# A grouped 1x1 convolution on one core: wider block transposes with longer write runs, and loads cut into four transfers

## The chip, the cores and the metric

One core of a Trainium2 chip runs the whole program. Times are device microseconds (us) of one execution. A run is in state fast or slow where several executions of the same kernel show which it was, and unknown for a single look; a single look therefore carries no claim of a per cent or less here.

## The reference

The input is an image of 512x512 pixels with 192 channels in bf16. The channels form 4 groups of 48, and each group of each pixel is multiplied by its own 48x48 matrix.

```python
H = W = 512; G = 4; Cg = 48; C = 192; k = 1          # x: (1, 512, 512, 192), w: (1, 1, 4, 48, 48)
xg = xp.reshape(B, H + 2 * pad, W + 2 * pad, G, Cg)  # pad = 0
out = out + jnp.einsum('bhwgc,gcd->bhwgd', xg[:, i:i+H, j:j+W, :, :], w[i, j])
```

100.7 MB are read and 100.7 MB written, whatever the kernel does.

## The kernel before

The kernel gives TensorE the channels on the partitions, but a pixel's channels lie side by side in memory. So pixels are loaded onto the partitions, VectorE transposes them in blocks of 32x32 (`Q` in the kernel), TensorE multiplies, ScalarE copies the result from PSUM into the same ring, and the ring is stored. A "column" is 128 pixels. A "piece" of up to 128 columns is one load and one store, and the ring holds 512 columns.

```python
# SP: a piece goes in two transfers (u); r and b together are the 128 partitions, b neighbouring ones
src = pixels(xf, p).rearrange("(r u b n) c -> u r b (n c)", r=64, u=2, b=2)
half = p.size * C // 2
for u in range(2):
    sp.dma_start(region(p)[:, u * half:(u + 1) * half], src[u]).then_inc(ld_sem[p.i], 16)
...
# VectorE: 8 columns per transpose
src = columns(s).rearrange("p (w v) g n -> p w v (g n)", w=2, v=2)
dst = xT[s % NXT][:].rearrange("p (b w i v) -> p w v b i", w=2, i=2, v=2)
dve.transpose(dst, src).then_inc(t_done, 1)
...
# TensorE: 12 matmuls per step of 8 columns, into one of two halves of PSUM
ins = pe.matmul(o, lhsT=xs[:, at:at + 128], rhs=r, start=(b == 1), stop=(b == 2), skip_group_check=True)
...
# ScalarE: one copy per step; a piece is stored in rows of 12 KB once its last step is done
act.copy(dst, src).then_inc(o_done, 1)
```

The load and the transpose are coupled. The 128 pixel columns of a matmul must come out in the order of the store, so the order in which pixels are loaded onto the lanes fixes the addresses to which a transpose writes. Here the innermost write loop is `i`: two bf16 elements, two elements (4 bytes) apart, and the next pair starts 16 bytes after the first.

Of the kernel before, what the change touches and what calls it, by code (L numbers as in the profile page):

```python
# [10 lines left out]
C = GROUPS * CG  # L11
Q = 32
NQ = 128 // Q
HC = C // 2
BLK = HC // Q
STEP = 8
XT = STEP * C
SEG = NQ * CG
WT = 8 * SEG

BIG = 128
RCOLS = 512
HEAD = (8, 8, 16, 32, 64)
TAIL = (64, 32, 16, 8, 8)
NXT = 4
ST_DELAY = 1


class Waiter:
# [21 lines left out]

def plan_pieces(cols):
    sizes = []
    if cols >= sum(HEAD) + sum(TAIL):
        mid = cols - sum(HEAD) - sum(TAIL)
        sizes = list(HEAD) + [BIG] * (mid // BIG) + ([mid % BIG] if mid % BIG else []) + list(TAIL)
    else:
        sizes = [BIG] * (cols // BIG) + ([cols % BIG] if cols % BIG else [])
    pieces, c = [], 0
    while sizes:  # L60
        s = min(sizes[0], RCOLS - c % RCOLS)
        sizes[0] -= s
        if not sizes[0]:
            sizes.pop(0)
        pieces.append(Piece(len(pieces), c, s))
        c += s
    return pieces


def bass_standalone__grouped__vision_kernel(nc, x, w, out):  # L70
    B, H, W_, Cx = x.shape
    assert Cx == C and tuple(w.shape) == (1, 1, GROUPS, CG, CG)
    npix = B * H * W_
    assert npix % (128 * STEP) == 0, "the pixel count must be a multiple of 1024"

    cols = npix // 128
    NS = cols // STEP
    pieces = plan_pieces(cols)
    piece_of = {s: p for p in pieces for s in range(p.s0, p.s1)}
    first = {p.s0: p for p in pieces}  # L80
    last = {p.s1 - 1: p for p in pieces}

    xf = x.rearrange("b h w c -> (b h w) c")
    of = out.rearrange("b h w c -> (b h w) c")
    wr = w.rearrange("a b g c d -> (a b g c) d")

    def pixels(ap, p):
        return ap[128 * p.col:128 * (p.col + p.size), :]

    with ExitStack() as es:  # L90
        block = es.enter_context(nc.Block())
        ring = es.enter_context(nc.sbuf_tensor("ring", [128, RCOLS * C], BF16))
        xT = [es.enter_context(nc.sbuf_tensor(f"xT{i}", [128, XT], BF16)) for i in range(NXT)]
        w_sb = es.enter_context(nc.sbuf_tensor("w_sb", [Q, 8, CG], BF16))
        wt = es.enter_context(nc.sbuf_tensor("wt", [128, WT], BF16))
        o_ps = es.enter_context(nc.psum_tensor("o_ps", [128, 8, 512], F32))

        def sem(name):
            return es.enter_context(nc.semaphore(name))

        ld_sem = [sem(f"ld{p.i}") for p in pieces]
        st_sem = [sem(f"st{p.i}") for p in pieces]
        w_sem, wz_sem, tz_sem, wc_sem = (sem(s) for s in ("w_sem", "wz_sem", "tz_sem", "wc_sem"))
        t_done, mm_done, o_done = sem("t_done"), sem("mm_done"), sem("o_done")

        def region(p):
            return ring[:, p.at * C:(p.at + p.size) * C]

        def columns(s):
            p = piece_of[s]  # L110
            g = (s - p.s0) * 2
            return region(p).rearrange("p (u g c) -> p u g c", u=NQ, g=p.run)[:, :, g:g + 2, :]

        @block.gpsimd
        def _(gp):
            gp.memset(w_sb[:], 0.0).then_inc(wz_sem, 1)  # L116
            gp.memset(wt[:], 0.0).then_inc(tz_sem, 1)  # L117

        @block.sync
        def _(sp):  # L120
            wq = Waiter(sp)
            for p in pieces:
                for q in pieces:
                    if q.col < p.col + p.size - RCOLS and q.col + q.size > p.col - RCOLS:
                        wq.wait(st_sem[q.i], 16)
                src = pixels(xf, p).rearrange("(r u b n) c -> u r b (n c)", r=64, u=2, b=2)
                half = p.size * C // 2
                for u in range(2):
                    sp.dma_start(region(p)[:, u * half:(u + 1) * half], src[u]).then_inc(ld_sem[p.i], 16)  # L129

        @block.vector
        def _(dve):
            wq = Waiter(dve)
            for s in range(NS):
                if s in first:
                    wq.wait(ld_sem[first[s].i], 32)
                wq.wait(mm_done, s - NXT + 1)
                src = columns(s).rearrange("p (w v) g n -> p w v (g n)", w=2, v=2)
                dst = xT[s % NXT][:].rearrange("p (b w i v) -> p w v b i", w=2, i=2, v=2)
                dve.transpose(dst, src).then_inc(t_done, 1)  # L140

        @block.tensor
        def _(pe):
            wq = Waiter(pe)
            wq.wait(wc_sem, NQ)
            for s in range(NS):
                wq.wait(t_done, s + 1)
                wq.wait(o_done, s - 1)
                xs = xT[s % NXT]
                ins = None  # L150
                for gh in range(4):
                    bank = o_ps[:, s % 2 * 4 + gh, 0:NQ * HC]
                    h = gh % 2
                    wh = wt[:, h * 4 * SEG:(h + 1) * 4 * SEG]
                    by_seg = bank.rearrange("p (a s c) -> p s a c", a=NQ, s=2)
                    for b, o, r in (
                        (1, by_seg, wh[:, 2 * SEG:4 * SEG].rearrange("p (s a c) -> p s a c", s=2, a=NQ)),
                        (0, by_seg[:, 0], wh[:, 0:SEG].rearrange("p (a c) -> p a c", a=NQ)),
                        (2, by_seg[:, 1], wh[:, SEG:2 * SEG].rearrange("p (a c) -> p a c", a=NQ)),
                    ):  # L160
                        at = (gh * BLK + b) * 128
                        ins = pe.matmul(o, lhsT=xs[:, at:at + 128], rhs=r, start=(b == 1), stop=(b == 2),  # L162
                                        skip_group_check=True)
                ins.then_inc(mm_done, 1)

        @block.scalar
        def _(act):
            wq = Waiter(act)
            wq.wait(wz_sem, 1)
            w4 = wr.rearrange("(h b j) d -> j h b d", h=2, b=BLK)  # L170
            s4 = w_sb[:].rearrange("p (h s) d -> p h s d", h=2)
            for b, j0, j1, seg in ((0, 0, Q, 0), (2, 0, Q, 1), (1, 0, 16, 2), (1, 16, Q, 3)):
                act.dma_start(s4[j0:j1, :, seg, :], w4[j0:j1, :, b, :]).then_inc(w_sem, 16)
            wq.wait(tz_sem, 1)
            wq.wait(w_sem, 64)
            for a in range(NQ):
                dst = wt[a * Q:(a + 1) * Q, :].rearrange("p (s a c) -> p s a c", s=8, a=NQ)[:, :, a, :]
                act.copy(dst, w_sb[:]).then_inc(wc_sem, 1)  # L178

            pending = []  # L180

            def store(p):
                wq.wait(o_done, p.s1)
                dst = pixels(of, p).rearrange("(a q g) c -> q a (g c)", a=NQ, q=128)
                src = region(p).rearrange("p (a n) -> p a n", a=NQ)
                act.dma_start(dst, src).then_inc(st_sem[p.i], 16)

            for s in range(NS):
                wq.wait(mm_done, s + 1)
                src = o_ps[:, s % 2 * 4:s % 2 * 4 + 4, 0:NQ * HC].rearrange("p b (a c) -> p b a c", a=NQ)  # L190
                dst = columns(s).rearrange("p a g (h c) -> p (g h) a c", h=2)
                act.copy(dst, src).then_inc(o_done, 1)  # L192
                if s in last:
                    pending.append(last[s])
                while pending and pending[0].s1 - 1 + ST_DELAY <= s:
                    store(pending.pop(0))
            for p in pending:
                store(p)
            for p in pieces:
                wq.wait(st_sem[p.i], 16)  # L200


# [26 lines left out]
```

## Time and profile before

The median was 887.16 us in three runs (886.97 to 888.39).

| what | value | view |
|---|---|---|
| VectorE busy | 874.4 of 885.2 us (99%) | busy times |
| one transpose, start to start | 3.414 us | chain in order of time |
| DMA engines busy | 27.9 + 27.3 + 0.2 = 55.4% | queue table |
| TensorE, ScalarE busy | 43%, 42% | busy times |

The page of the kernel before: busy times with their share of the span, then the DMA share in 40 slices (tenths; 9 is 90% or more) with the GB/s, the queues (packets, MB, share of the 16 engines' span; q1 is the loads, q10 the stores), the chain that ended last, and the costliest group of instructions.

```profile
PE 382.2 (43%) x3072; PEld 257.4 (29%) x3072; DVE 874.4 (99%) x256; ACT 371.8 (42%) x261; POOL 1.9 (0%) x6
...
DMA  8998457193671926629266391763908542060444
GB/s 335 432 421 343 178 249 321 54 374 143 275 294 80 378 113 284 285 105 377 89 285 284 131 381 59 303 267 159 380 32 329 241 182 103 1 284 1 203 184 183
...
q1 hardware_dynamic: 6912, 100.67, 27.9%
q10 hardware_dynamic: 12928, 100.68, 27.3%
...
DVE 95%; issue 4%; DVEq 1%; DMA 0%; PE 0%; ACT 0%; SPq 0%
...
L140 DVE STREAM_TRANSPOSE xT<-ring 128x1536 bf16<-128x1536 bf16 x256 | 874.4, 3617 | 4.6 <-DMA ring<-in_x_dram 4.6
```

VectorE has almost no idle time (it waited 4.6 us), and the chain is its transposes. The DMA row shows idle stretches throughout, with values near 430 GB/s only at the start, when the ring is first filled.

The chain in order of time (start us, length us, what):

```profile
106.99 53.01 DVE xT L140 x16
159.99 1.62 issue
161.62 53.01 DVE xT L140 x16
```

Sixteen transposes start every 161.62 - 106.99 = 54.63 us, hence 3.414 us each. The mean of 3617 ns in the group is longer because neighbours overlap.

A stretch of the fill (start:end, length, busy us of PE, PEld, DVE, ACT and POOL with instruction counts, granted clock, DMA share, GB/s).

```profile
20.00:60.00 40.00, 16.89 (x137) 11.45 (x138) 40.00 (x13) 17.15 (x12) 0.00 (x0) 1.00 1.01 429
```

### The profile page before, as it was taken

How to read it: one execution, taken by the hardware profiler on the slowest of the kernel's cores; microseconds unless marked ns; L12 is line 12 of the kernel's file. 1: busy time of each engine (PE TensorE's matmuls, PEld its weight loads, DVE VectorE, ACT ScalarE, POOL GpSimd, SP SyncE). 2: the span in 40 equal slices, each digit the busy share in tenths (PEclk: the TensorE clock that was granted, in tenths of full speed). 3: DMA queues.
4: the chain of work that ended last, by engine and by line, in shares of the span. 5: the costliest groups of instructions: out<-in, count | busy, mean ns of one | idle time of the engine just before them, and what ended most of it. 6: DMA issues, size and time to landing. Idle time of an engine off the chain costs nothing.

```text
span 885.2 us, 7058 instructions
## 1 busy us (share of the span) xinstructions
PE 382.2 (43%) x3072; PEld 257.4 (29%) x3072; DVE 874.4 (99%) x256; ACT 371.8 (42%) x261; POOL 1.9 (0%) x6
## 2 busy tenths in 40 slices
PE   3444444444444444444444444444444444444443
PEld 2323232323232323222222223232323232323232
DVE  7999999999999999999999999999999999999997
ACT  4444434343434344444444444444443434343433
POOL 0000000000000000000000000000000000000000
PEclk9999999999999999999999999999999999999999
DMA  8998457193671926629266391763908542060444
GB/s 335 432 421 343 178 249 321 54 374 143 275 294 80 378 113 284 285 105 377 89 285 284 131 381 59 303 267 159 380 32 329 241 182 103 1 284 1 203 184 183
DMA packets 19869, 201.79 MB, mean 228 GB/s; under 512 B 1408, under 2 KB 5504, under 8 KB 8576
## 3 DMA queue, kind: packets, MB, share of 16 engines
q1 hardware_dynamic: 6912, 100.67, 27.9%
q10 hardware_dynamic: 12928, 100.68, 27.3%
q8 instruction: 25, 0.41, 0.2%
q14 instruction: 4, 0.03, 0.0%
HBM read 100.68 MB, written 100.66 MB: 227 GB/s over the span
## 4 chain that ended last, share of the span: by engine, by line
DVE 95%; issue 4%; DVEq 1%; DMA 0%; PE 0%; ACT 0%; SPq 0%
DVE xT L140 95%; DVEq L90 1%; DMA ring<-in_x_dram 0%; PE o_ps L162 0%; ACT ring L192 0%; SPq L129 0%
## 5 line engine op out<-in xcount | busy, mean ns | idle before, releaser
L140 DVE STREAM_TRANSPOSE xT<-ring 128x1536 bf16<-128x1536 bf16 x256 | 874.4, 3617 | 4.6 <-DMA ring<-in_x_dram 4.6
L162 PE MATMUL o_ps<-wt,xT 128*128 128x192 bf16 (+1 forms) x3072 | 382.2, 275 | 498.4 <-DVE xT L140 488.6
L192 ACT CAST ring<-o_ps 128x1536 bf16<-128x1536 f32 x256 | 368.4, 1440 | 503.9 <-PE o_ps L162 499.8
L162 PEld LDWEIGHTS o_ps<-wt,xT 128*128 128x128 bf16 x3072 | 257.4, 98 | 622.9 <-DVE xT L140 545.8
L178 ACT ACT_TABLE_LOAD x1 | 1.3, 1283 | 6.3 <-DMA w_sb<-in_w_dram 6.3
L178 ACT COPY wt<-w_sb 32x384 bf16<-32x384 bf16 x4 | 2.0, 510 | 0.1
L117 POOL MEMSET wt<- 128x1536 bf16 x1 | 1.4, 1372 | 0.0
L116 POOL MEMSET w_sb<- 32x384 bf16 x1 | 0.4, 407 | 0.3 <-POOLq L214 0.3
L214 POOL MEMSET const-bfloat16-1.0<- 128x1 bf16 x1 | 0.1, 103 | 0.0
L214 POOL MEMSET const-uint8-127<- 128x1 uint8 x1 | 0.1, 103 | 0.0
L214 POOL MEMSET const-float32-0.0<- 128x1 f32 x1 | 0.1, 98 | 0.2 <-issue 0.2
L214 POOL MEMSET const-float32-1.0<- 128x1 f32 x1 | 0.1, 98 | 0.0
## 6 DMA issues: line engine op xcount, KB each, us to landing
ring<-in_x_dram SPq DMA_DIRECT2D x28, 3072.0 KB, 17.4
out_dram<-ring ACTq DMA_DIRECT2D x14, 6144.0 KB, 16.5
ring<-in_x_dram SPq DMA_DIRECT2D x4, 1536.0 KB, 10.8
out_dram<-ring ACTq DMA_DIRECT2D x2, 3072.0 KB, 12.8
ring<-in_x_dram SPq DMA_DIRECT2D x4, 768.0 KB, 9.9
out_dram<-ring ACTq DMA_DIRECT2D x2, 1536.0 KB, 21.3
ring<-in_x_dram SPq DMA_DIRECT2D x8, 192.0 KB, 8.0
ring<-in_x_dram SPq DMA_DIRECT2D x4, 384.0 KB, 9.2
```

The costliest lines, as they stand in the source:

```text
L90: with ExitStack() as es:
L116: gp.memset(w_sb[:], 0.0).then_inc(wz_sem, 1)
L117: gp.memset(wt[:], 0.0).then_inc(tz_sem, 1)
L140: dve.transpose(dst, src).then_inc(t_done, 1)
L162: ins = pe.matmul(o, lhsT=xs[:, at:at + 128], rhs=r, start=(b == 1), stop=(b == 2), skip_group_check=True)
L178: act.copy(dst, w_sb[:]).then_inc(wc_sem, 1)
L192: act.copy(dst, src).then_inc(o_done, 1)
L214: nc = _bacc.Bacc("TRN2", target_bir_lowering=False, num_devices=1)
```

## The change

It makes a transpose 16 columns wide and rearranges the load so that a transpose can write 8 neighbouring pixels side by side. For that, a load is cut into four transfers with rows of 12 KB, and its partitions form 16 blocks of 8 neighbours instead of 64 blocks of 2. The taper of small pieces at the end is dropped; instead, the last piece's store goes in three parts.

```diff
-XT = STEP * C
+WIDE = 16
+XT = WIDE * C
-TAIL = (64, 32, 16, 8, 8)
-NXT = 4
-ST_DELAY = 1
+LAST_PARTS = (16, 8, 8)
+NXT = 2
...
-                src = pixels(xf, p).rearrange("(r u b n) c -> u r b (n c)", r=64, u=2, b=2)
-                half = p.size * C // 2
-                for u in range(2):
+                src = pixels(xf, p).rearrange("(r u b n) c -> u r b (n c)", r=16, u=NQ, b=8)
+                part = p.size * C // NQ
+                for u in range(NQ):
...
-                src = columns(s).rearrange("p (w v) g n -> p w v (g n)", w=2, v=2)
-                dst = xT[s % NXT][:].rearrange("p (b w i v) -> p w v b i", w=2, i=2, v=2)
+                src = columns(s, n).rearrange("p u g n -> p u (g n)")
+                dst = xT[d % NXT][:, 0:n * STEP * C].rearrange("p (b r u i) -> p u b r i", r=4, u=NQ, i=8)
...  # TensorE takes two steps from one transpose; the store list is cut for the last piece
```

More of the change, by code (lines that the diff above doesn't have):

```diff
@@ L53, in plan_pieces @@
     sizes = []
-    if cols >= sum(HEAD) + sum(TAIL):
-        mid = cols - sum(HEAD) - sum(TAIL)
-        sizes = list(HEAD) + [BIG] * (mid // BIG) + ([mid % BIG] if mid % BIG else []) + list(TAIL)
+    if cols >= sum(HEAD) + BIG:
+        mid = cols - sum(HEAD)
+        sizes = list(HEAD) + [BIG] * (mid // BIG) + ([mid % BIG] if mid % BIG else [])
     else:
@@ L80, in bass_standalone__grouped__vision_kernel @@
     first = {p.s0: p for p in pieces}
-    last = {p.s1 - 1: p for p in pieces}
+    ops = [range(s, min(s + WIDE // STEP, p.s1)) for p in pieces for s in range(p.s0, p.s1, WIDE // STEP)]
+    op_of = {s: d for d, steps in enumerate(ops) for s in steps}
     xf = x.rearrange("b h w c -> (b h w) c")
@@ L107, in region, with columns @@
             return ring[:, p.at * C:(p.at + p.size) * C]
-        def columns(s):
+        def columns(s, n=1):
             p = piece_of[s]
             g = (s - p.s0) * 2
-            return region(p).rearrange("p (u g c) -> p u g c", u=NQ, g=p.run)[:, :, g:g + 2, :]
+            return region(p).rearrange("p (u g c) -> p u g c", u=NQ, g=p.run)[:, :, g:g + 2 * n, :]
         @block.gpsimd
@@ L125, in _ @@
                         wq.wait(st_sem[q.i], 16)
-                src = pixels(xf, p).rearrange("(r u b n) c -> u r b (n c)", r=64, u=2, b=2)
-                half = p.size * C // 2
-                for u in range(2):
-                    sp.dma_start(region(p)[:, u * half:(u + 1) * half], src[u]).then_inc(ld_sem[p.i], 16)
+                src = pixels(xf, p).rearrange("(r u b n) c -> u r b (n c)", r=16, u=NQ, b=8)
+                part = p.size * C // NQ
+                for u in range(NQ):
+                    sp.dma_start(region(p)[:, u * part:(u + 1) * part], src[u]).then_inc(ld_sem[p.i], 16)
         @block.vector
@@ L133, in _ @@
             wq = Waiter(dve)
-            for s in range(NS):
+            for d, steps in enumerate(ops):
+                s, n = steps[0], len(steps)
                 if s in first:
-                    wq.wait(ld_sem[first[s].i], 32)
-                wq.wait(mm_done, s - NXT + 1)
-                src = columns(s).rearrange("p (w v) g n -> p w v (g n)", w=2, v=2)
-                dst = xT[s % NXT][:].rearrange("p (b w i v) -> p w v b i", w=2, i=2, v=2)
+                    wq.wait(ld_sem[first[s].i], 16 * NQ)
+                if d >= NXT:
+                    wq.wait(mm_done, ops[d - NXT][-1] + 1)
+                src = columns(s, n).rearrange("p u g n -> p u (g n)")
+                dst = xT[d % NXT][:, 0:n * STEP * C].rearrange("p (b r u i) -> p u b r i", r=4, u=NQ, i=8)
                 dve.transpose(dst, src).then_inc(t_done, 1)
@@ L146, in _ @@
             for s in range(NS):
-                wq.wait(t_done, s + 1)
+                d = op_of[s]
+                wq.wait(t_done, d + 1)
                 wq.wait(o_done, s - 1)
-                xs = xT[s % NXT]
+                xs = xT[d % NXT][:, (s - ops[d][0]) * STEP * C:]
                 ins = None
@@ L178, in _, with store @@
                 act.copy(dst, w_sb[:]).then_inc(wc_sem, 1)
-            pending = []
-            def store(p):
-                wq.wait(o_done, p.s1)
-                dst = pixels(of, p).rearrange("(a q g) c -> q a (g c)", a=NQ, q=128)
-                src = region(p).rearrange("p (a n) -> p a n", a=NQ)
+            todo = []
+            for p in pieces:
+                g0 = 0
+                for n in LAST_PARTS if p is pieces[-1] and p.run == sum(LAST_PARTS) else (p.run,):
+                    todo.append((p, g0, g0 + n, p.s0 + (g0 + n) // 2))
+                    g0 += n
+            st_val = {p: 16 * sum(q is p for q, *_ in todo) for p in pieces}
+            def store():
+                p, g0, g1, s1 = todo.pop(0)
+                wq.wait(o_done, s1)
+                dst = pixels(of, p).rearrange("(a q g) c -> q a (g c)", a=NQ, q=128)[:, :, g0 * C:g1 * C]
+                src = region(p).rearrange("p (a n) -> p a n", a=NQ)[:, :, g0 * C:g1 * C]
                 act.dma_start(dst, src).then_inc(st_sem[p.i], 16)
@@ L192, in _ @@
                 act.copy(dst, src).then_inc(o_done, 1)
-                if s in last:
-                    pending.append(last[s])
-                while pending and pending[0].s1 - 1 + ST_DELAY <= s:
-                    store(pending.pop(0))
-            for p in pending:
-                store(p)
+                while todo and todo[0][3] <= s:
+                    store()
+            while todo:
+                store()
             for p in pieces:
-                wq.wait(st_sem[p.i], 16)
+                wq.wait(st_sem[p.i], st_val[p])
 _INS = ['x', 'w']
```

## The prediction

> **What bounds the kernel now.** VectorE's transposes. The page gives VectorE 99% busy (874.4 us, 256 transposes of 128x1536, mean 3617 ns); the chain that ended last is 95% that line. In the chain in order of time 16 transposes start every 54.63 us (106.99 to 161.62): 3.414 us from start to start, 874 us for 256. TensorE and ScalarE wait for transposes (488.6 and 499.8 us in the waits); VectorE waited 4.6 us in all. The DMA engines are busy 55.4% of 885.2 us = 490 us (queue table: 27.9 + 27.3 + 0.2) for 201.8 MB.
>
> **What the change does.**
>
> 1. Transposes: 128 of 128x3072 instead of 256 of 128x1536. [...] I read the old cost as a write penalty: each element goes alone into half of a 4-byte word. [...] the old writes touch two words but fill neither (that this is what hurts is my inference; no run shows it yet). New writes are 8 adjacent bf16. [...] VectorE saves about 445 us, all of it critical until another limit binds.
> 2. Other limits. ScalarE: 256 x 1.44 = 369 us plus store issues. TensorE and ScalarE over two PSUM halves: (1.52 + 1.44 + 0.05) / 2 = 1.5 us a step, 385 us (estimate from the timeline). DMA: 490 us. So DMA becomes the bound.
> 3. Loads: four transfers of 12 KB rows instead of two of 24 KB. The stores already have 12 KB rows and cost the same engine time for the same bytes (27.3% against 27.9%), so the load's engine time should stay within 3%. Issues double (0.6 us each), hidden except 1 to 2 us before the first transpose.
> 4. Tail: the last piece is 128 columns, its store cut 16/8/8. After the last transpose come two steps and a store of 1.5 MB, about 8 us more exposed.
>
> **Time.** DMA 490 us, 2 us before it starts, 10 to 15 us of tail, and 10 to 20 us of gaps and mixed-direction losses (6 MB alone takes 17.4 us to load, 16.5 to store; in series 33.9 us a piece, 16 pieces 542 us; overlapped less): 525 us. Range 488 to 620[...]. Chances: faster by over 2% 0.93, within 2% 0.05, slower 0.02.
>
> **What would show each step right or wrong.**
> - Groups by form: 128 transposes of 128x3072, mean 3.3 to 3.7 us. At 6.6 us, step 1 is wrong and the total about 860 us.
> - VectorE's share 80 to 88%, with tens of us of waits for the ring's DMA; DMA 9 in nearly all 40 slices, 380 to 430 GB/s; the chain mostly DMA.
> - Queue table: the load queue's share times the span still about 247 us.
> - ScalarE 370 us and TensorE 380 us busy, unchanged.
>
> **What would make it wrong.** [...] Or loads and stores together reach well under 400 GB/s: 540 to 580 us. Or the ring of four pieces leaves DMA gaps between a store's landing and the next load.

In step 1 the sum of the 128 new transposes came to 430 us, and the 445 us saved are the 874 us of the old ones less that. What would make it wrong was that a transpose keeps its old time per element whatever the writes, for a gain of only 1 to 3%. All of these were my estimates, shown by nothing measured. The sum of 525 us is the DMA's 490 us with start, tail and gaps.

## The result, and the profile after

The median was 546.71 us (542.77 to 553.14 in four runs, one of them slow), against 887.07 us for the kernel before. The ratio is 0.6146, 95% interval 0.6102 to 0.6191. A ratio here is the mean time of one kernel's fast runs over that of the other's of the same rounds, so not quite the ratio of the medians.

The page of the kernel after, the same lines:

```profile
PE 387.8 (71%) x3072; PEld 280.1 (51%) x3072; DVE 421.2 (77%) x129; ACT 361.3 (66%) x261; POOL 1.9 (0%) x6
...
DMA  6999999999999999999999999999999999999698
GB/s 176 271 251 243 258 257 281 298 406 411 393 412 395 394 383 418 423 344 430 384 428 382 397 427 426 426 377 428 367 423 416 421 419 329 427 398 427 255 413 339
...
q1 hardware_dynamic: 11520, 100.67, 52.5%
q10 hardware_dynamic: 11872, 100.68, 46.0%
...
DMA 55%; another core or an unknown queue 19%; DVE 10%; SPq 10%; PE 3%; DVEq 1%; issue 1%; ACT 1%
DMA ring<-in_x_dram 35%; DMA out_dram<-ring 20%; DVE xT L143 10%; SPq L130 10%; PE o_ps L166 3%; DVEq L91 1%; ACT ring L203 1%; SPq L39 0%
```

The groups by form and the waits of the kernel after (waits: engine, line, for what: us in total, times, longest us):

```profile
L143 DVE STREAM_TRANSPOSE xT<-ring 128x3072 bf16<-128x3072 bf16 x127 | 417.6, 3346 | 107.6 <-DMA ring<-in_x_dram 88.3 <-PE o_ps L166 19.2
```

```profile
DVE xT L143 <- DMA ring<-in_x_dram: 94.4, 20, 16.2
DVE xT L143 <- PE o_ps L166: 19.2, 13, 2.1
```

A transpose of twice the width now takes less time than a narrow one did: 3346 against 3617 ns. VectorE is busy for 421.2 us instead of 874.4 and waits 94.4 us for loads. The DMA row is 9 almost everywhere, so the DMA bounds the kernel, as predicted.

Two lines do not fit the prediction. The load queue took 52.5% of 547.1 us = 287 us of the engines' time, not 247. And the first eight slices (110 us) move only 176 to 298 GB/s although the engines are busy all the time from the second slice on. The same stretch as shown for before:

```profile
20.00:60.00 40.00, 20.31 (x144) 14.27 (x144) 19.06 (x7) 18.33 (x13) 0.00 (x0) 0.78 1.03 252
```

Before moved 429 GB/s here, after 252, both at a DMA share of about 1. These rates count both directions; the load queue's own packets came to 415 GB/s before and 230 after. The engines are not idle; their packets take longer: in the middle of the fill (40 to 50 us) a 12 KB packet of the load took 820 ns (median).

### The profile page after: what moved, and what is told of

The parts are those of the page before. It is cut to its first block, busy times and chain, and to the rows that moved or that the text cites. A ratio compares the mean times of both kernels' runs of the same rounds, so it can differ in the third digit from the quotient of the medians.

```text
span 547.1 us, 6829 instructions
## 1 busy us (share of the span) xinstructions
PE 387.8 (71%) x3072; PEld 280.1 (51%) x3072; DVE 421.2 (77%) x129; ACT 361.3 (66%) x261; POOL 1.9 (0%) x6
## 3 DMA queue, kind: packets, MB, share of 16 engines
q1 hardware_dynamic: 11520, 100.67, 52.5%
## 4 chain that ended last, share of the span: by engine, by line
DMA 55%; another core or an unknown queue 19%; DVE 10%; SPq 10%; PE 3%; DVEq 1%; issue 1%; ACT 1%
DMA ring<-in_x_dram 35%; DMA out_dram<-ring 20%; DVE xT L143 10%; SPq L130 10%; PE o_ps L166 3%; DVEq L91 1%; ACT ring L203 1%; SPq L39 0%
## 5 line engine op out<-in xcount | busy, mean ns | idle before, releaser
L143 DVE STREAM_TRANSPOSE xT<-ring 128x3072 bf16<-128x3072 bf16 (+1 forms) x129 | 421.2, 3321 | 113.6 <-DMA ring<-in_x_dram 94.4
L166 PE MATMUL o_ps<-wt,xT 128*128 128x192 bf16 (+1 forms) x3072 | 387.8, 287 | 149.9 <-DVE xT L143 139.7
L203 ACT CAST ring<-o_ps 128x1536 bf16<-128x1536 f32 x256 | 358.0, 1441 | 172.3 <-PE o_ps L166 171.5
L166 PEld LDWEIGHTS o_ps<-wt,xT 128*128 128x128 bf16 x3072 | 280.1, 103 | 257.3 <-DVE xT L143 165.1
```

## The experiments

Two questions were open: what made the transposes twice as fast, and what made the loads slow. All kernels below are the kernel after with two numbers set free: LANES, the neighbouring partitions of a block (8 in the kernel after), and SEGS (1).

```diff
+LANES = 8
+SEGS = 1
-src = pixels(xf, p).rearrange("(r u b n) c -> u r b (n c)", r=16, u=NQ, b=8)
+src = pixels(xf, p).rearrange("(r u b n) c -> u r b (n c)", r=128 // LANES, u=NQ // SEGS, b=LANES)
-dst = ....rearrange("p (b r u i) -> p u b r i", r=4, u=NQ, i=8)                       # SEGS = 1
+dst = ....rearrange("p (b r u i) -> p u b r i", r=32 // LANES, u=NQ, i=LANES)
+dst = ....rearrange("p (b u i v) -> p u v b i", u=NQ // SEGS, i=LANES, v=SEGS)        # SEGS = 2
```

With SEGS = 1 a load has four transfers of 12 KB rows, and a transpose writes LANES neighbouring bf16 (2 bytes apart) before it hops. With SEGS = 2 a load has two transfers of 24 KB rows, and the LANES elements of a run lie 4 bytes apart, each in half of a 4-byte word. LANES = 2, SEGS = 2 is the layout of the kernel before.

### Width alone, layout alone

old_layout_wide:

```diff
-LANES = 8
-SEGS = 1
+LANES = 2
+SEGS = 2
```

> The kernel after, but with the old layout: loads of two transfers with 24 KB rows (64 outer blocks of 2 partitions), and each transpose writing pairs of bf16 two elements apart, now 16 columns wide. Theory W (the writes cost the time): 128 transposes of 128x3072 at 6.5 to 6.8 us each, total 850 to 880 us. Rival C (the number of instructions cost it): about 3.4 us each, total near 545 us or less. Loads: all theories say 400 GB/s or more from 20 to 60 us.

Measured: 894.09 us (one look), 14 us above the expected range. By-form group:

```profile
L145 DVE STREAM_TRANSPOSE xT<-ring 128x3072 bf16<-128x3072 bf16 x127 | 867.7, 7029 | 1.3 <-PE o_ps L168 1.3
```

The wide transpose with the old writes takes 7029 ns, twice the new one. From start to start it is 867.7 / 127 = 6.83 us, just above the 6.5 to 6.8 us that theory W expected and twice the 3.414 us of the narrow one. Width does nothing for the rate. The loads moved 433 GB/s from 20 to 60 us, as all theories said.

new_layout_narrow:

```diff
-WIDE = 16
-NXT = 2
+WIDE = 8
+NXT = 4
```

> The kernel after, but with 8 columns per transpose (256 of 128x1536, four buffers) and the new layout. Theory W: about 1.7 us from start to start, mean about 1.8 us, total within 2% of the kernel after (535 to 560 us). Rival C: 3.4 us from start to start, total near 880 us. Loads: as in the kernel after, 225 to 285 GB/s from 20 to 60 us.

Measured: 549.03 us (one look). By-form group of new_layout_narrow:

```profile
L145 DVE STREAM_TRANSPOSE xT<-ring 128x1536 bf16<-128x1536 bf16 x256 | 427.3, 1740 | 108.2 <-DMA ring<-in_x_dram 108.2
```

Half the width with the new layout costs 1740 ns. In its timeline 16 such transposes take 26.68 us, so (26.68 - 1.74) / 15 = 1.663 us from start to start; 6 wide ones of the kernel after take 19.68 us, (19.68 - 3.35) / 5 = 3.266 us. The width is worth 2 x 1.663 - 3.266 = 0.06 us per 16 columns, about 8 us of VectorE time over the kernel, and VectorE is no longer the bound. Rival C falls: the layout did it.

### What the loads lost

Theory P, here and below, is that the split of the 128 partitions into blocks slows the load.

runs_of_4:

```diff
-LANES = 8
+LANES = 4
```

> The kernel after with 4 adjacent bf16 per write run instead of 8, which also makes a load 32 outer blocks of 4 partitions (still four transfers of 12 KB rows). Transposes: if two full 4-byte words side by side are enough, 3.3 to 3.4 us each; if it takes 16 bytes, over 4.5 us. Loads: theory P[...] says over 400 GB/s from 20 to 60 us and a total of 495 to 515 us. Rivals R (12 KB rows are slow to load) and N (four transfers and their many descriptors are slow) say 225 to 285 GB/s as in the kernel after, and a total of 540 to 555 us.

Measured: 493.0 us median (492.75 to 493.66, four fast runs), ratio to before 0.556 (0.555 to 0.5569). It beats the kernel after by 54 us and lies 2 us below the range that theory P gave. Its by-form group, then the window 20 to 60 us:

```profile
L145 DVE STREAM_TRANSPOSE xT<-ring 128x3072 bf16<-128x3072 bf16 x127 | 416.6, 3343 | 52.9 <-DMA ring<-in_x_dram 38.1 <-PE o_ps L168 14.8
```

```profile
20.00:60.00 40.00, 31.86 (x245) 22.89 (x246) 33.60 (x11) 27.63 (x20) 0.00 (x0) 0.91 1.02 425
```

The transposes are unchanged (3343 ns), so the 54 us come from the layout of the loads. The load still has four transfers of 12 KB rows, and the window is now as fast as before: 425 GB/s (382 of them the load queue's own), and 460 ns for the same 12 KB packet. Rivals R (row size) and N (number of transfers) fall. The DMA rows of its page:

```profile
GB/s 184 387 424 426 424 426 427 429 429 429 429 429 430 427 428 429 428 429 429 430 428 428 430 430 426 429 430 430 427 430 427 427 429 428 431 429 275 289 409 329
...
q1 hardware_dynamic: 11520, 100.67, 48.8%
```

From the third slice on it moves 424 GB/s or more nearly to the end. The load queue's time is 48.8% of 491.1 = 240 us.

rows_24k_lanes_8:

```diff
-SEGS = 1
+SEGS = 2
```

> The kernel after with two load transfers of 24 KB rows again, but in 16 outer blocks of 8 partitions; a transpose then writes 8 bf16 two elements apart. Loads from 20 to 60 us: theory P says 225 to 285 GB/s, rivals R and N say over 400. Transposes: if half-filled words are what costs, about 6.5 us each and a total of 850 to 890 us; if the hop after each two writes is what costs, 3.3 to 3.5 us.

Measured: 657.96 us (one look). Its window and by-form group:

```profile
20.00:60.00 40.00, 11.47 (x84) 8.23 (x81) 13.11 (x4) 8.47 (x7) 0.00 (x0) 0.68 1.02 225
```

```profile
L145 DVE STREAM_TRANSPOSE xT<-ring 128x3072 bf16<-128x3072 bf16 x127 | 424.3, 3409 | 207.1 <-DMA ring<-in_x_dram 120.8 <-PE o_ps L168 86.4
```

Rows of 24 KB in two transfers are slow again (225 GB/s) as soon as the blocks have 8 partitions. So the blocks matter. (The later phase, loads and stores together, also ran at only 323 GB/s from 120 to 600 us here, which none of the theories foresaw; why is open.) The transposes were a surprise: 3409 ns with every word only half filled. That speaks against the inference of my prediction, half-filled words as the cost.

runs_of_16 and eight_other_rows tried to say why blocks of 8 are slow. Under theory P it is the split of the partitions over the DMA engines; the picture of that split, from which P took its 105 to 120 GB/s for runs_of_16, was not shown by any run. Rival E is that a load with 8 outer blocks runs on 8 engines, and that only their number counts.

```diff
-LANES = 8
+LANES = 16          # runs_of_16
```

> The kernel after with 8 outer blocks of 16 partitions in each load (runs of 16 in the writes, 12 KB rows, four transfers). [...] Theory P[...]:[...] loads from 20 to 60 us at 105 to 120 GB/s and a total over 800 us. Rival E (only the number of engines counts, and blocks of 8 were slow for another reason): about 200 to 230 GB/s, total 550 to 660 us. Transposes 3.3 to 3.4 us under both.

Measured: 749.43 us (one look). The queue lines and the window of runs_of_16:

```profile
q1 hardware_dynamic: 10880, 100.67, 32.7%
q10 hardware_dynamic: 11872, 100.68, 32.4%
```

```profile
20.00:60.00 40.00, 22.92 (x156) 16.09 (x154) 19.91 (x6) 18.31 (x13) 0.00 (x0) 0.74 0.60 215
```

The loads are 20 pieces x 4 transfers x 128 rows = 10240 packets of data. The kernel after had 11520 - 10240 = 1280 more, packets of 4 bytes, 16 for each of the 80 transfers; here it is 10880 - 10240 = 640, 8 each. I read this as 8 outer blocks on 8 engines, where 16 blocks had 16; that is an inference, since the traces count the packets but do not name their engine. The rate, 215 GB/s with stores in it, does not fit P: the load queue's own packets come to 156 GB/s from 20 to 60 us and 169 from 60 to 100, where P expected 105 to 120. After the fill a 12 KB packet of the load takes 460 ns (median from 120 to 600 us; 580 from 20 to 60 us, 464 from 60 to 100), no more than the 460 ns in runs_of_4. So what P expected is refuted for blocks of 16.

The rival's total, 550 to 660 us, is missed too. A possible reason, estimated from the queue lines: if all loads ran on the same eight engines and the stores evenly on all sixteen, each of the eight spent 2 x 32.7% of 747.6 = 489 us on loads and 32.4% = 242 us on stores, 731 of 747.6 us (an estimate; the kept traces do not name the engine of a packet). Eight full engines would then be the bound, at a DMA share that reads only 0.60 in the window; VectorE waited 285.8 us for loads in this run.

```diff
-"(r u b n) c -> u r b (n c)"      # eight_other_rows
+"(u b r n) c -> u r b (n c)"
```

> Wrong result on purpose. The kernel after, its loads still four transfers of 16 outer blocks of 8 partitions with 12 KB rows, but the rows come from DRAM in another order: each transfer reads one whole stretch of 1.5 MB[...]. Theory P (the split of the 128 partitions over the engines slows the load, whatever the addresses in DRAM): again 225 to 285 GB/s from 20 to 60 us, total 535 to 560 us. Rival D (the order of the addresses in DRAM slows it): over 380 GB/s from 20 to 60 us and a total under 510 us. Transposes 3.3 to 3.4 us under both.

Measured: 541.03 us (one look), result wrong as intended. Its window:

```profile
20.00:60.00 40.00, 19.32 (x144) 13.87 (x144) 20.16 (x7) 18.22 (x13) 0.00 (x0) 0.83 1.03 266
```

With quite another order of addresses in DRAM, blocks of 8 load as slowly: 266 GB/s. This order at least is not the cause. Within the fill of the kernel after, moreover, pieces of 16 to 128 columns, whose DRAM strides differ eightfold, were all slow: 220 to 260 GB/s for the load queue's own packets, summed over 1.5 MB at a time.

### Which writes are fast

A "line" below is a name for 16 bytes of a partition, starting at a multiple of 16 (the buffers themselves are taken to start at one); whether it is the unit that counts is what these runs test. Theory L says that writes are fast only when at least four in a row fall into one line; theory F, that half-filled words are slow.

runs_of_2:

```diff
-LANES = 8
+LANES = 2
```

> 12 KB rows in four transfers, 64 outer blocks of 2 partitions; each transpose writes 2 adjacent bf16 (one full 4-byte word), then hops. Theory L[...]: two per line again, so 6.5 to 7.0 us per transpose as with the old pairs, total 860 to 900 us. Theory F (half-filled words cost): words are full, 3.3 to 3.5 us. Loads from 20 to 60 us: over 400 GB/s[...].

Measured: 492.57 us (one look). By-form group:

```profile
L145 DVE STREAM_TRANSPOSE xT<-ring 128x3072 bf16<-128x3072 bf16 x127 | 416.6, 3343 | 53.0 <-DMA ring<-in_x_dram 37.0 <-PE o_ps L168 16.0
```

Its window:

```profile
20.00:60.00 40.00, 31.42 (x243) 22.70 (x242) 33.22 (x11) 27.27 (x20) 0.00 (x0) 0.91 1.02 425
```

Blocks of 2 load as fast as blocks of 4 (425 GB/s). Two neighbouring bf16, one full word, then a hop: full speed (3343 ns). Theory L, at least four writes per 16-byte line, falls. Theory F explains this one, but not rows_24k_lanes_8.

rows_24k_lanes_4 and lanes_4_shifted:

```diff
-LANES = 8
-SEGS = 1
+LANES = 4
+SEGS = 2
 # lanes_4_shifted only: the buffers start 8 bytes later
-xT = [... "xT{i}", [128, XT], BF16)) for i in range(NXT)]
+xT = [... "xT{i}", [128, XT + 8], BF16))[:, 4:4 + XT] for i in range(NXT)]
```

> 24 KB rows in two transfers, 32 outer blocks of 4 partitions; each transpose writes 4 bf16 two elements apart: half-filled words, all four inside one 16-byte line. Theory L: 3.3 to 3.45 us per transpose. Theory F: over 6 us. Theory P: loads over 400 GB/s from 20 to 60 us, total 485 to 497 us, a few us below runs_of_4 (493) because the first loads need half the issues. Rival H (blocks of 4 were fast only because of their 12 KB rows): total over 505 us.

> The same as rows_24k_lanes_4 with the transposed buffers 8 bytes further on, so that each group of four writes falls two and two into neighbouring 16-byte lines. Theory L: 6.5 to 7.0 us per transpose, total 860 to 900 us. Rival J (what costs is the jump over skipped addresses, at most one per four writes is free): 3.3 to 3.5 us, total as rows_24k_lanes_4.

Measured: 496.64 us (496.11 to 496.86, four fast runs) and 894.48 us (one look). Group and window of rows_24k_lanes_4, then the group of lanes_4_shifted:

```profile
L145 DVE STREAM_TRANSPOSE xT<-ring 128x3072 bf16<-128x3072 bf16 x127 | 424.1, 3414 | 44.0 <-PE o_ps L168 33.8 <-DMA ring<-in_x_dram 10.2
20.00:60.00 40.00, 23.00 (x173) 16.25 (x170) 25.33 (x8) 18.41 (x13) 0.00 (x0) 0.83 1.01 432
```

```profile
L145 DVE STREAM_TRANSPOSE xT<-ring 128x3072 bf16<-128x3072 bf16 x127 | 868.0, 7056 | 0.7 <-PE o_ps L168 0.7
```

Four half-filled words inside one 16-byte line are fast (3414 ns); the same four writes split two and two over neighbouring lines take 7056 ns. Only the buffers' start differs. Rival J, the jump over skipped addresses, falls. So does rival H: with 24 KB rows blocks of 4 load at 432 GB/s. But the total is 3.6 us above runs_of_4, not a few us below as expected. The first loads come faster, but the DMA row of rows_24k_lanes_4 dips later in the fill:

```profile
GB/s 272 433 434 427 428 409 277 410 422 261 426 424 438 424 429 419 428 434 420 430 433 417 425 426 430 433 424 429 423 428 429 433 425 422 430 430 423 425 407 197
```

The slices at 277 and 261 GB/s lack about 9 us of transfer at 427 GB/s (estimate), more than the 3.6 us by which it is behind; what causes them was not looked into.

runs_of_8_odd and runs_of_2_odd move the buffers of the kernel after and of runs_of_2 by 2 bytes:

```diff
-xT = [... "xT{i}", [128, XT], BF16)) for i in range(NXT)]
+xT = [... "xT{i}", [128, XT + 8], BF16))[:, 1:1 + XT] for i in range(NXT)]
```

Theory M was written in cycles of a clock that no run here shows. In ns (an estimate): a line that gets a half-filled word costs at least as much as two elements of the old layout, 2 x 3.414 us / 1536 = 4.45 ns (kernel before), and a line with only full words costs its elements, 3.266 us / 3072 = 1.063 ns each (kernel after). A run of 8 that is off by 2 bytes then takes 7 x 1.063 + 4.45 = 11.9 ns, and the 384 runs of a transpose 4.56 us.

> The kernel after with the transposed buffers 2 bytes further on: each run of 8 bf16 covers 3 full words, a half word at each end, and 7 + 1 elements in two 16-byte lines. Theory M[...]:[...] about 4.5 to 4.8 us per transpose. Rival S (only adjacency of the writes counts): 3.3 to 3.5 us. Total then 620 to 660 us under M, 540 to 560 under S.

> runs_of_2 with the transposed buffers 2 bytes further on: each pair of adjacent bf16 now half-fills two neighbouring words of one line instead of filling one. Theory M: 6.6 to 7.1 us per transpose as with the old pairs, total 860 to 900 us. Rival S: 3.3 to 3.5 us, total about 493 us as runs_of_2.

Measured: 560.20 us and 894.68 us (one look each). Groups of runs_of_8_odd, then of runs_of_2_odd:

```profile
L145 DVE STREAM_TRANSPOSE xT<-ring 128x3072 bf16<-128x3072 bf16 x127 | 517.5, 4260 | 20.0 <-DMA ring<-in_x_dram 18.7 <-PE o_ps L168 1.2
```

```profile
L145 DVE STREAM_TRANSPOSE xT<-ring 128x3072 bf16<-128x3072 bf16 x127 | 868.4, 7038 | 0.0
```

Neighbouring writes are not enough (rival S falls): two bytes of offset double the time of runs of 2 (7038 against 3343 ns). Theory M gets the direction and runs_of_2_odd right, but not the size of runs_of_8_odd: 4260 ns instead of 4500 to 4800. In its timeline 118 transposes take 480.05 us, (480.05 - 4.26) / 117 = 4.07 us from start to start. That is 4.07 us / 384 = 10.6 ns per run of 8, where M wanted 11.9. The total missed its range (620 to 660) for the same reason.

| a run of bf16 writes, then a hop | in words and 16-byte lines | transpose, ns |
|---|---|---|
| 2, 4 bytes apart (before's layout, wide) | 2 half words, one line | 7029 |
| 2 neighbours, off by 2 bytes | 2 half words, one line | 7038 |
| 4, 4 bytes apart, off by 8 bytes | 2 half words in each of two lines | 7056 |
| 8 neighbours, off by 2 bytes | 3 full and 2 half words, 7 + 1 in two lines | 4260 |
| 4, 4 bytes apart | 4 half words, one line | 3414 |
| 8, 4 bytes apart | 4 half words in each of two lines | 3409 |
| 2, 4, 8 or 16 neighbours | full words only | 3343, 3343, 3346, 3347 |

What the rows agree with: full words are fast (3343 to 3347 ns), and half words are fast when four of them follow each other in one 16-byte line (3409 and 3414 ns); two in a line are slow (7029 to 7056 ns). The run of 8 that is off by 2 bytes lies in between (4260 ns), and this rule does not give its size. The mechanism behind it was not settled.

### A try at the end of the kernel

short_tail is rows_24k_lanes_4 with a taper again:

```diff
+TAIL = (64, 32, 16, 16)          # and plan_pieces puts it at the end
```

> rows_24k_lanes_4 with the last 128 columns as pieces of 64, 32, 16 and 16 instead of one piece stored in three parts. If the 10 us dip of the DMA near the end (110 GB/s from 450 to 460 us in runs_of_4) comes from the store waiting for the last large piece to land and be computed, 4 to 10 us less than rows_24k_lanes_4, total 477 to 490 us. If it comes from something else, the same within 3 us.

Measured: 496.97 us (496.24 to 497.80, four fast runs), the same as rows_24k_lanes_4. The expectation rested on the dip at 450 to 460 us in runs_of_4, and rows_24k_lanes_4 has no such dip (425 GB/s there), so this run could not tell. runs_of_4 stays the best kernel timed in rounds.

## Why the prediction was right or wrong

The measured 546.7 us lie in the range of 488 to 620, 22 us above the 525 of the sum.

1. "128 transposes of 128x3072, mean 3.3 to 3.7 us": right. They took 3346 ns, and VectorE 421 us in all against the 430 of the sum. The inference under step 1, that half-filled words are what hurts, was only part of the truth: rows_24k_lanes_8 and rows_24k_lanes_4 fill no word in a run and are fast (3409 and 3414 ns). Half words cost when only two of them share a 16-byte line (7029 to 7056 ns), and in part when a line holds one (4260 ns in runs_of_8_odd). The doubt that a transpose might keep its old time per element whatever the writes is settled: twice the width took 3.266 us from start to start with the new writes, against 6.83 us with the old.
2. "DMA becomes the bound": right. The chain is 55% DMA (another 19% has a releaser that the profile can't name), VectorE waits 94.4 us for loads and the DMA row is 9. VectorE's share fell to 77%, just under the predicted 80 to 88%, because the span was longer.
3. "The load's engine time should stay within 3%": this step failed. It measured 287 us instead of 247, 16% more. The argument was that stores with 12 KB rows cost no more than loads with 24 KB rows. Row size turned out not to matter (runs_of_4: 240 us with the same rows). What mattered is the thing that the prediction read past in the diff: blocks of 8 neighbouring partitions instead of 2.
4. The tail: "about 8 us more exposed". The last transpose ended 12 us before the end of the span in the kernel after and 6 us before, so about 6 us more (508.61 + 26.20 = 534.8 of 547.1 us in the timeline, against 848.04 + 30.99 = 879.0 of 885.2). Right in size.
5. "10 to 20 us of gaps and mixed-direction losses": smaller in the best kernel. runs_of_4 moves loads and stores together at 424 to 431 GB/s for most of its span; its two slices at 275 and 289 GB/s lack about 8 us (estimate).

That the total came out only 22 us off is in part luck. The queues of the kernel after took 52.5 + 46.0 + 0.3 = 98.8% of 547.1 = 540.5 us of the engines' time where the sum had 490 (40 us more for loads, 10 for stores), and left 6.6 us idle where the sum allowed 35 for start, tail and gaps: 50 too few and 28 too many. The total also falls among the "540 to 580 us" that the prediction gave for loads and stores staying well under 400 GB/s together. That is not what happened: together they reached 404 GB/s from 120 to 500 us, and the slow part was the fill, which is nearly all load.

Where the 54 us between the kernel after and runs_of_4 lie, estimated from the windows: in the first 120 us the kernel after moves 267 GB/s on average, 32.0 MB. runs_of_4 moves 253 for 20 us, 426 for 80 and 429 for 20, 47.7 MB. The difference at 429 GB/s is 37 us. The rest is mostly the mixed phase, 404 against 429 GB/s.

Still open is why blocks of 8 partitions slow a load with few stores beside it so much: its own packets moved 230 GB/s against 382 with blocks of 4 in 12 KB rows, 214 against 415 in 24 KB rows (20 to 60 us). It is shown that it is not the row size, not the number of transfers, and not the one other order of DRAM addresses that was tried. Theory P's picture of the split failed at runs_of_16 (156 GB/s where it expected 105 to 120), so no mechanism is shown. The kept traces name neither engine nor partition of a packet and can't decide it, and no run dealt 16 blocks out to other partitions.

## What to carry to other kernels

When the order of a load is rearranged to suit an engine, look at how the outermost dimension of the transfer splits over the partitions: here blocks of 2 or 4 loaded at 425 GB/s or more, blocks of 8 at 225 to 266, while the DMA share read 1.0 in both. So read GB/s beside the share, first in a stretch where only one direction runs. For writes of bf16 with a stride, choose the shortest run that fills whole 4-byte words, since longer runs bought nothing here (3343 ns with runs of 2, 3347 with runs of 16) and forced the block size of the load, and keep it aligned: two bytes of offset cost 27% (runs of 8) to 110% (runs of 2).
